# The first head pair's spectral weights in 4,096-byte rows of two modes, shared out over the slots anew, and the inverse transform's matrix made later

## The chip, the cores and the metric

The kernel runs on one core of a Trainium2 chip. The metric is the device time of one execution in microseconds. An execution that the hardware profiler took gives the profile; its span runs from the first to the last instruction of the program.

## The reference

Sliding-window attention with a linear bias per head feeds a spectral mixing layer:

```
scores = q @ k.T / 8 - slope[h] * |i - j|     kept where 0 <= i - j < 128
x = softmax(scores) @ v                       8 batches, 8 heads, 576 positions, 64 wide -> (8, 576, 512)
X = rfft(x, axis=1)[:, :64]                   64 modes
Y[b, m] = X[b, m] @ (w_r[m] + i w_i[m])       a 512 x 512 complex matrix for each mode
u = x + irfft(Y)
out = u + relu(u @ w_ch)
```

All inputs and the output are fp32. `w_r` and `w_i` have 64 x 512 x 512 elements each: 1 MiB for one mode of one of them, 134 MB in all, which is most of what the kernel reads.

## The kernel before, in words

Two heads are a pair: 128 of the 512 channels. A unit is one pair of one batch. `GROUPS` has two groups: pair 0 alone (8 units, one for each batch), then pairs 1, 2 and 3 together (24 units). Units are numbered 0 to 31 in this order. The program for each engine is in the order in which the code issues it; nothing is rescheduled.

The first stage is a run of slots, `_slot(g, n, w0, w1)`. In slot n PE does the scores of unit n (L407), the transposes of q and k of unit n + 1 (L381), a part of the modes' products (`w0`), the remaining scores, the spectrum of unit n - 2 (L502), then the attention-value product of unit n - 1 (L460), and last the other part of the modes (`w1`). ScalarE takes the exponentials (L419) and evicts the transposes (L389), VectorE multiplies by masks and normalizes, GpSimd casts q, k (L364) and v (L371) and issues the loads of v (L340). SyncE issues all other loads, in order: q and k of unit n + 8 in slot n (L329), and weights (L567).

The spectrum is a product with a matrix `F` of cosines and sines. Its result for a group goes to `X[j]`, with channels on partitions, in the three planes -imaginary, real, imaginary.

The products of pair 0 with its weights (`_modes`, L602 for `wr` and L606 for `wi`) run within the slots of the second group's attention and two slots (`TAIL`) behind them. A weight tile has three modes (22 tiles, the last with one): for a mode 128 rows of 512 fp32 elements, 2,048 contiguous bytes, one row to a partition. The tiles stand in a ring of three buffers for `wr` and three for `wi`. A tile is loaded when the tile three before it is used up; the load is issued in the same slot. The tiles are spread evenly from slot 10 on: one in each of slots 10 to 15, 17 to 21, 23 to 28 and 30 to 34. The result is added up in one PSUM tile for 8 modes, and ScalarE copies it to `ZTa` (L615).

`FT` is the matrix of the inverse transform, used only in the finish. `_ft(g, c)` makes a quarter of it: the first call transposes `F` (L308), scales it (L309), and each call makes a permutation `order` on GpSimd (L313), multiplies by it (L317) and evicts the result with ScalarE (L319). The calls stand behind slots 27 to 30.

Then comes the last stage: for each of 64 modes a tile with the rows of pairs 1, 2 and 3 (6,144 contiguous bytes to a partition, 768 KB for each of `wr` and `wi`), in the same ring; its products, and between them the transposes of x and x @ `w_ch` (`_xt` L628, `_xw` L637). The finish (`_finish`) applies `FT`, adds up and stores.

Of the kernel before, what the change touches and what calls it, by code (L numbers as in the profile page):

```python
# [9 lines left out]
FP32 = mybir.dt.float32  # L10
# [11 lines left out]
ROWS = 3  # L22
LV = 3
QK = 9
TAIL = 2


# [5 lines left out]
def kernel(  # L33
# [35 lines left out]


    g.FT = persist.tile([P, 4, S], BF16)
    g.ident_b = persist.tile([P, P], BF16)
    g.ident2 = persist.tile([P, 64], BF16)
    g.wch = persist.tile([P, 4, DM], BF16)
# [11 lines left out]
    with tc.manual_schedule(engines={ET.SP, ET.PE, ET.Activation, ET.DVE, ET.Pool}):  # L86
        with ExitStack() as wctx:
# [4 lines left out]
            with ExitStack() as actx:  # L92
                cp = actx.enter_context(tc.tile_pool(name="const", bufs=1))
                for j, grp in enumerate(GROUPS[:-1]):
                    g.X[j] = cp.tile([P, len(grp), 3, B, NM], BF16, name=f"X{j}")
                g.F = cp.tile([P, ST, P], BF16)
# [48 lines left out]

                line = [(j, *t) for j in range(len(GROUPS)) for t in tiles[j]]
                ahead = RING
                work = {n: [] for n in range(N + 2 + TAIL)}
                for j in range(len(GROUPS) - 1):
                    per = g.first[j + 2] - g.first[j + 1] + (TAIL if j + 2 == len(GROUPS) else 0)  # L150
                    for i, t in enumerate(tiles[j]):
                        work[g.first[j + 1] + 2 + i * per // len(tiles[j])].append((j, *t))
                for n in range(3, N + 2 + TAIL):
                    if g.first[1] <= n and loaded < N:
                        _load_unit(g, loaded)
                        loaded += 1
                    w = work[n]
                    for _ in w:
                        _load_w(g, *line[ahead])
                        ahead += 1  # L160
                    h = (len(w) + 1) // 2
                    _slot(g, n, w[:h], w[h:])
                    if N - 5 <= n < N - 1:
                        _ft(g, n - N + 5)
                    for i in range(2):
                        if n == g.first[1] + 4 + 4 * i:
                            _load_wch(g, i)
                        if n == g.first[1] + 6 + 4 * i:
                            _cast_wch(g, i)
# [8 lines left out]
            with ExitStack() as xctx:  # L178
# [30 lines left out]
def _consts(g, tp):  # L209
# [13 lines left out]
    for vb in g.vbs:  # L223
        nc.gpsimd.memset(vb[:, :, g.D : g.D + 1], 1.0)
    nc.gpsimd.memset(g.vbt[:, :, :, g.D : g.D + 1], 1.0)


    pcol = tp.tile([P, 1], FP32)
# [41 lines left out]
        nc.vector.tensor_tensor(out=r, in0=r, in1=o, op=ALU.max)  # L270
    nc.vector.tensor_scalar(off, rel, float(P), FAR, op0=ALU.is_ge, op1=ALU.mult)
    nc.vector.tensor_tensor(out=rel, in0=rel, in1=off, op=ALU.max)
    for s in range(g.NP):
        nc.vector.memset(slope[0:64, s : s + 1], -(2.0 ** (-8.0 * (2 * s + 1) / g.H)))
        nc.vector.memset(slope[64:128, s : s + 1], -(2.0 ** (-8.0 * (2 * s + 2) / g.H)))
# [15 lines left out]
    return 3 if k == c else c if k == 3 else k  # L291


def _ft(g, c):


    nc = g.nc
    S = g.S
    if c == 0:
        cvec = g.work.tile([P, 1], FP32, tag="cvec", name="cvec", bufs=1)  # L300
# [3 lines left out]
        g.FTn = g.work.tile([P, S], BF16, tag="FTn", name="FTn", bufs=1)  # L304
        for st in range(g.ST):
            n = min(P, S - st * P)
            tp = g.ps1.tile([P, P], BF16, tag="tqk", name="tft")
            nc.tensor.transpose(tp[:, 0:n], g.F[0:n, st], g.ident_b[0:n, 0:n])  # L308
            nc.vector.tensor_scalar_mul(g.FTn[:, st * P : st * P + n], tp[:, 0:n], cvec)  # L309
    order = g.work.tile([P, P], BF16, tag="order", name="order", bufs=1)  # L310
    src = g.ident_b.rearrange("p (r g m) -> p g r m", r=2, g=4)
    for k in range(4):
        nc.gpsimd.tensor_copy(  # L313
            order[:, 32 * k : 32 * k + 32].rearrange("p (r m) -> p r m", r=2), src[:, _block(c, k)])
    for a, z in ((0, 512), (512, S)):
        ps = g.ps1.tile([P, 512], FP32, tag="sc", name="ftp")
        nc.tensor.matmul(  # L317
            ps[:, 0 : z - a], lhsT=order, rhs=g.FTn[:, a:z], start=True, stop=True)
        nc.scalar.copy(g.FT[:, c, a:z], ps[:, 0 : z - a])  # L319
# [158 lines left out]
def _spectrum(g, n):  # L478
# [10 lines left out]
    po = 64 * (b % 2)  # L489
    ps = slice(po, po + 64)  # L490
    X = g.X[j]
    nb = 4 // A
    if b % nb == 0:
        g.xt = g.ps2.tile([P, nb, A, 2, g.NM], FP32, tag="xt", name="xt")
# [10 lines left out]
    if b % nb == nb - 1:  # L505
# [5 lines left out]
        for a in range(A):  # L511
            xi = xt[:, :, a].rearrange("p b i m -> p i b m")
            nc.vector.tensor_copy(X[:, a, 1:3, b0 : b0 + nb], xi)
            nc.vector.tensor_scalar_mul(X[:, a, 0, b0 : b0 + nb], xi[:, 1], -1.0)


def _slot(g, n, w0, w1):
# [32 lines left out]
        _spectrum(g, n - 2)  # L550
    if 0 <= n - 1 < N:
        _av(g, n - 1)
    if n < N:
        _mask3(g, n)
    for w in w1:
# [3 lines left out]
def _load_w(g, j, m0, mg):  # L559
# [3 lines left out]
    t = []  # L563
    for tag, src in (("wr", g.w_r), ("wi", g.w_i)):
        w = g.wpool.tile([P, ROWS, g.DM], FP32, tag=tag, name=f"{tag}{j}_{m0}")
        w = w[:, 0 : mg * A].rearrange("p (m a) e -> p m a e", a=A)
        nc.sync.dma_start(  # L567
            out=w.rearrange("p m a e -> p m (a e)"),
            in_=src[m0 : m0 + mg, rows].rearrange("m (p a) e -> p m (a e)", a=A))
        t.append(w)  # L570
    for i in range(mg):
        g.W[j, m0 + i] = (t[0][:, i], t[1][:, i])

# [12 lines left out]
def _modes(g, j, m0, n, last=False):  # L586
# [3 lines left out]
    X = g.X[j]  # L590
    A = len(GROUPS[j])
    ends = set(range(MB, g.NM + 1, MB)) | ({g.NM - 4, g.NM - 2} if last else set())
    for m in range(m0, m0 + n):
        if m == 0 or m in ends:
            g.acc[j] = (m, g.mpsum.tile([P, 4, 2, MB, 8], FP32, tag="acc", name="acc"))
# [20 lines left out]
        else:  # L616
            o = dst
            if last:
                o = g.ZT[:, :, c0 // 16, :, c0 % 16 : m % 16 + 1, :].rearrange(
                    "p e a m b -> p e a (m b)")  # L620
            nc.vector.tensor_tensor(out=o, in0=acc, in1=dst, op=ALU.add)


def _xt(g, n, pool, psum):
# [183 lines left out]
```

## Time and the profile before

| | |
|---|---|
| median of 3 runs | 493.46 us (493.18 to 494.25) |
| profiled execution | 492.82 us, span 491.1 us, mean granted clock of TensorE 0.782 |
| busy in the span | PE 372.5, VectorE 232.7, ScalarE 186.7, GpSimd 150.0 us |
| moved | 173.99 MB, 354 GB/s mean |
| weight transfers | 85 + 85 of 768 KB, 1 + 1 of 256 KB |

In the slices of the profile each digit is the busy share of an engine in tenths; PEclk is the clock that TensorE was granted, in tenths of full speed; DMA is the mean busy share of the core's 16 DMA engines. In the stretches the numbers behind an engine are busy microseconds and instructions, then come the granted clock, the DMA share (two queues that overlap can make it more than 1) and GB/s. In SyncE's waits the numbers are the microseconds in all, how often, and the longest.

### The profile page before, as it was taken

To read this page: it belongs to the slowest core of one execution; us is meant where nothing else is said; L and a number is where in the kernel's file an instruction comes from. 1 tells how busy PE (TensorE), PEld (TensorE's weight loads), DVE (VectorE), ACT (ScalarE), POOL (GpSimd) and SP (SyncE) were. 2 spreads that over 40 slices of the span, in tenths; PEclk is the share of its full clock that TensorE was granted. 3 is DMA by queue.
4 is the path that set the end of the run, shared out by engine and by line. 5 is a ranking of instruction groups with operands and counts; after the bars stand their busy time and mean duration, and the time that the engine had idled before them with its cause. 6 is when DMAs were issued, how large, how long until landed. Compare 5 with 4: busy or idle time off the path is not lost.

```text
span 491.1 us, 14883 instructions
## 1 busy us (share of the span) xinstructions
PE 372.5 (76%) x6415; PEld 252.9 (52%) x6415; DVE 232.7 (47%) x494; ACT 186.7 (38%) x343; POOL 150.0 (31%) x230
## 2 busy tenths in 40 slices
PE   2585787697677878777878798778868798845983
PEld 2464676576566756544544454444435455523542
DVE  8487663755745655532333334233332343202984
ACT  3694654655555547221111221222111132102772
POOL 8798673392935423000000000000000000000995
PEclk9988775967767569578787778888798788555999
DMA  8999999999999975799999999999999999992677
GB/s 251 299 295 283 328 291 350 355 363 343 362 377 311 361 294 178 247 410 424 423 423 423 424 423 423 423 424 418 420 415 424 423 424 421 424 423 104 223 288 258
DMA packets 54050, 173.99 MB, mean 354 GB/s; under 512 B 5600, under 2 KB 5600, under 8 KB 53984
## 3 DMA queue, kind: packets, MB, share of 16 engines
q1 hardware_dynamic: 50528, 163.60, 87.6%
q0 software_dynamic: 3456, 9.44, 7.4%
q8 instruction: 50, 0.82, 0.6%
q14 instruction: 16, 0.13, 0.1%
HBM read 163.58 MB, written 9.44 MB: 352 GB/s over the span
## 4 chain that ended last, share of the span: by engine, by line
DMA 60%; PE 25%; issue 6%; DVE 3%; ACT 3%; POOL 1%; SPq 1%; DVEq 0%; ACTq 0%; POOLq 0%
DMA wi<-in_moe_w_i_dram 53%; PE sc L407 5%; PE av L460 4%; DMA q<-in_q_dram 3%; PE acc L606 3%; PE xt L502 3%; DMA wchf<-in_moe_w_ch_dram 3%; PE acc L602 3%; PE tqk L381 3%; PE mm L637 2%; PE tp L628 1%; DVE r L766 1%; POOL o L774 1%; ACT att L419 1%; PE y L637 1%
## 5 line engine op out<-in xcount | busy, mean ns | idle before, releaser
L774 POOL TENSOR_TENSOR o<-r,ys 128x512 f32<-128x512 f32 x25 | 30.8, 1266 | 262.6 <-ACT ys L765 262.6
L655 ACT CAST hl<-xw 128x512 bf16<-128x512 f32 x72 | 42.1, 585 | 154.5 <-PE xw L637 150.2
L637 PE MATMUL xw<-wch,xT 128*64 128x512 bf16 x576 | 93.8, 465 | 0.0
L419 ACT ACTIVATE att<-sc 128x512 bf16<-128x512 f32 (+1 forms) x128 | 72.4, 592 | 53.8 <-PE sc L407 53.3
L606 PEld LDWEIGHTS <-wi 128*128 128x128 bf16 x1024 | 65.8, 103 | 52.1 <-DMA wi<-in_moe_w_i_dram 47.1
L602 PEld LDWEIGHTS <-wr 128*128 128x128 bf16 x1024 | 67.1, 103 | 40.4 <-issue 24.7
L656 DVE TENSOR_TENSOR hl<-xw,hl 64x512 bf16<-64x512 f32 x72 | 50.0, 695 | 79.3 <-ACT hl L655 79.3
L606 PE MATMUL acc<-Xlast,wi 128*128 128x16 bf16 x768 | 55.3, 193 | 37.1 <-DMA wi<-in_moe_w_i_dram 37.1
L422 DVE TENSOR_TENSOR att<-att,mask 128x512 bf16<-128x512 bf16 x96 | 46.9, 510 | 52.2 <-ACT att L419 51.6
L407 PE MATMUL sc<-qkT,qkT 64*64 64x256 bf16 (+1 forms) x512 | 56.9, 335 | 16.6 <-ACT att L419 5.9
L602 PE MATMUL acc<-Xlast,wr 128*128 128x16 bf16 x768 | 59.4, 193 | 12.7 <-DMA wr<-in_moe_w_r_dram 10.1
L637 PEld LDWEIGHTS <-xT 128*64 128x64 bf16 x576 | 37.9, 132 | 38.8 <-issue 22.0
L407 PEld LDWEIGHTS <-qkT 64*64 64x64 bf16 x512 | 33.8, 131 | 26.4 <-issue 18.4
L381 PE MATMUL tqk<-ident_b,qkb 64*64 64x64 bf16 x1152 | 34.0, 216 | 15.2 <-POOL qkb L364 8.0
L389 ACT COPY qkT<-tqk 128x576 bf16<-128x576 bf16 x64 | 41.1, 645 | 6.3 <-PE tqk L381 6.3
L381 PEld LDWEIGHTS <-qkb 64*64 64x64 bf16 x1152 | 34.1, 131 | 16.5 <-POOL qkb L364 8.6
L340 POOL DMA_DIRECT2D v<-in_v_dram x64 | 39.5, 622 | 0.8 <-POOL vb L371 0.8
L630 DVE COPY xT<-tp 128x512 bf16<-128x512 bf16 x36 | 15.3, 424 | 46.3 <-PE tp L628 45.9
L460 PE MATMUL av<-vb,att 64*128 64x65 bf16 (+1 forms) x1024 | 34.6, 221 | 3.3 <-issue 2.4
L460 PEld LDWEIGHTS <-att 64*128 64x128 bf16 (+1 forms) x1088 | 29.2, 116 | 8.3 <-issue 3.8
L371 POOL CAST vb<-v 128x512 bf16<-128x512 f32 x32 | 21.1, 658 | 39.3 <-PE av L460 37.9
L364 POOL CAST qkb<-q 128x576 bf16<-128x576 f32 x32 | 24.7, 771 | 6.4 <-PE tqk L381 4.9
(104 smaller groups left out, 486.4 us busy)
## 6 DMA issues: line engine op xcount, KB each, us to landing
wr<-in_moe_w_r_dram SPq DMA_DIRECT2D x85, 768.0 KB, 8.3
wi<-in_moe_w_i_dram SPq DMA_DIRECT2D x85, 768.0 KB, 9.7
q<-in_q_dram SPq DMA_DIRECT2D x32, 288.0 KB, 11.7
k<-in_k_dram SPq DMA_DIRECT2D x32, 288.0 KB, 11.4
v<-in_v_dram POOLq DMA_DIRECT2D x64, 128.0 KB, 7.3
out_dram<-o SPq DMA_DIRECT2D x32, 256.0 KB, 2.3
vt<-in_v_dram POOLq DMA_DIRECT2D x8, 128.0 KB, 8.2
wchf<-in_moe_w_ch_dram SPq DMA_DIRECT2D x2, 512.0 KB, 15.1
```

Source lines behind the costliest of these rows:

```text
L340: g.nc.gpsimd.dma_start(out=u.v[64 * hh : 64 * hh + 64].rearrange("p t r d -> p t (r d)"), in_=g.v[b, 2 * s + hh, 0:512, :].rearrange("(t ...
L381: g.nc.tensor.transpose(tp[hs, r, :], u.b[w][hs, r], g.ident_b[hs, hs], tile_position=(64 * hh, 64 * hh))
L389: g.nc.scalar.copy(dst.rearrange("c (p r) -> c p r", r=g.R), u.tp[w].rearrange("c r p -> c p r"))
L407: nc.tensor.matmul(sc[hs, r * nq : (r + 1) * nq], lhsT=kT[hs, kt * P + r : kt * P + P : 2], rhs=qT[hs, kt * P : kt * P + nq], start=True, ...
L419: nc.scalar.activation(a[:, :cols], sc[:, :cols], AF.Exp, scale=1.0 / math.sqrt(g.D))
L422: nc.vector.tensor_tensor(out=a, in0=a, in1=g.mask[:, s], op=ALU.mult)
L460: nc.tensor.matmul(av[o, hh, col(t)], lhsT=a[hs, c0 : c0 + m], rhs=vb[hs, 0 : D + 1], start=(j == 0), stop=(j == len(terms) - 1), tile_pos ...
L602: nc.tensor.matmul(o, lhsT=wr[:, a].bitcast(BF16)[:, 1::2][:, c], rhs=X[:, a, 1:3, :, m], start=(a == 0), stop=False)
L606: nc.tensor.matmul(o, lhsT=wi[:, a].bitcast(BF16)[:, 1::2][:, c], rhs=X[:, a, 0:2, :, m], start=False, stop=(a == A - 1))
L637: nc.tensor.matmul(out[64 * h : 64 * h + 64], lhsT=lhsT[h], rhs=rhs[h], tile_position=(0, 64 * h), **kw)
L655: nc.scalar.copy(hl, xw)
L656: nc.vector.tensor_tensor(out=hl[64:128], in0=xw[64:128], in1=hl[64:128], op=ALU.subtract)
```

## The change

Three things change. First, the weights of pair 0 come as 32 tiles instead of 22. A tile has modes m and m + 32, and one transfer of 512 KB for each of `wr` and `wi` brings both: the even partitions hold mode m, the odd ones mode m + 32, and each partition has two neighbouring channels' rows, 4,096 contiguous bytes. The product contracts over all 128 partitions at once, so `X[0]` gets a form with zeros: for each of the two modes, the partitions of the other one are zero, and the result has 32 columns (two modes, real and imaginary, 8 batches) instead of 16. A tile has 16 products for two modes, as before. Since a channel's spectrum now has to stand on an even and on an odd partition, a product with a permutation `swap` exchanges neighbouring partitions, and `_place` writes both versions, multiplied by 0 or 1 (`par`), on VectorE and ScalarE; this is done twice, in slots 5 and 9, for four batches each. `ZTa` is filled by two copies for each four tiles.

Second, the tiles are shared out otherwise: a weight of 4 for each slot up to 23 and of 7 from slot 24 on. One tile goes to each of slots 10 to 20, 22, 23, 25, 28, 30, 33 and 35, two to each of slots 24, 26, 27, 29, 31, 32 and 34.

Third, the four calls of `_ft` move from behind slots 27 to 30 to the last stage, behind its tiles 4 to 7; `F` is kept for that long, and the PSUM buffers are those of that stage.

```diff
+SHARE, SHARE_END = 4, 7
...
-        tiles.append([(m, min(mg, NM - m)) for m in range(0, NM, mg)])
+        tiles.append([(m, min(mg, NM - m)) for m in range(0, NM, mg)] if len(grp) > 1 else
+                     [(m, 2) for m in range(NM // 2)])
...
-                    per = g.first[j + 2] - g.first[j + 1] + (TAIL if j + 2 == len(GROUPS) else 0)
+                    steps = []
+                    for n in range(g.first[j + 1] + 2, g.first[j + 2] + 2):
+                        steps += [n] * (SHARE if n < N - LA else SHARE_END)
+                    if j + 2 == len(GROUPS):
+                        steps += [n for n in range(N + 2, N + 2 + TAIL)] * SHARE_END
+                    steps.sort()
                     for i, t in enumerate(tiles[j]):
-                        work[g.first[j + 1] + 2 + i * per // len(tiles[j])].append((j, *t))
+                        work[steps[i * len(steps) // len(tiles[j])]].append((j, *t))
...
-                    if N - 5 <= n < N - 1:
-                        _ft(g, n - N + 5)
...
+                    if 5 <= done < 9:
+                        _ft(g, done - 5, xt, xps)
...
+def _spectrum_swap(g, j, b):
+
+    sw = g.ps1.tile([P, 4, 2, g.NM], FP32, tag="sc", name="sw")
+    g.nc.tensor.matmul(
+        sw.rearrange("p b r m -> p (b r m)"), lhsT=g.swap,
+        rhs=g.xn.rearrange("p b r m -> p (b r m)"), start=True, stop=True)
+    _place(g, j, b - 3, sw, 1)
+
+
+def _place(g, j, b0, src, d):
+
+
+    nc = g.nc
+    n = g.NM // 2
+    for i in range(2):
+        o = g.X[j][:, i ^ d, i, :, :, b0 : b0 + 4]
+        x = src[:, :, :, n * i : n * i + n].rearrange("p b r m -> p r m b")
+        if i == 0:
+            nc.vector.tensor_scalar_mul(o[:, 1:3], x, g.par[:, 0:1])
+            nc.vector.tensor_scalar_mul(o[:, 0], x[:, 1], g.par[:, 2:3])
+        else:
+            nc.scalar.mul(o[:, 1:3], x, g.par[:, 1:2])
+            nc.scalar.mul(o[:, 0], x[:, 1], g.par[:, 3:4])
...
+        if A == 1:
+            w = w[:, 0:2]
+            nc.sync.dma_start(
+                out=w.rearrange("p a e -> p (a e)"),
+                in_=src[m0 : m0 + g.NM // 2 + 1 : g.NM // 2, rows].rearrange(
+                    "m (p a) e -> p m (a e)", a=2))
+            t.append(w)
+            continue
...
+def _modes_pair(g, j, m0):
...
+    if m0 % 4 == 0:
+        g.acc[j] = g.mpsum.tile([P, 4, 2, 2, 4, 8], FP32, tag="acc", name="acc")
...
+        for a in range(2):
+            for w, r in ((wr, 1), (wi, 0)):
+                nc.tensor.matmul(
+                    acc[:, et, :, :, m0 % 4], lhsT=w[:, a].bitcast(BF16)[:, 1::2][:, c],
+                    rhs=X[:, a, :, r : r + 2, m0],
+                    start=(a == 0 and r == 1), stop=(a == 1 and r == 0))
+    if m0 % 4 == 3:
+        for i in range(2):
+            m = i * g.NM // 2 + m0 - 3
+            dst = g.ZTa[:, :, :, m : m + 4].rearrange("p e r m b -> p e r (m b)")
+            src = acc[:, :, i].rearrange("p e r m b -> p e r (m b)")
+            if j == 0:
+                nc.scalar.copy(dst, src)
```

More of the change, by code (lines that the diff above doesn't have):

```diff
@@ L71 @@
     g.FT = persist.tile([P, 4, S], BF16)
+    g.F = persist.tile([P, ST, P], BF16)
     g.ident_b = persist.tile([P, P], BF16)
@@ L94 @@
                 for j, grp in enumerate(GROUPS[:-1]):
-                    g.X[j] = cp.tile([P, len(grp), 3, B, NM], BF16, name=f"X{j}")
-                g.F = cp.tile([P, ST, P], BF16)
+                    shape = [2, 2, 3, NM // 2, B] if len(grp) == 1 else [len(grp), 3, B, NM]
+                    g.X[j] = cp.tile([P, *shape], BF16, name=f"X{j}")
+                g.swap = cp.tile([P, P], BF16)
+                g.par = cp.tile([P, 4], FP32)
                 g.mask = cp.tile([P, NP, 512], BF16)
@@ L225, in _consts @@
     nc.gpsimd.memset(g.vbt[:, :, :, g.D : g.D + 1], 1.0)
+    nc.gpsimd.tensor_copy(
+        g.swap.rearrange("p (a i) -> p i a", i=2)[:, 0],
+        g.ident_b.rearrange("p (a i) -> p i a", i=2)[:, 1])
+    nc.gpsimd.tensor_copy(
+        g.swap.rearrange("p (a i) -> p i a", i=2)[:, 1],
+        g.ident_b.rearrange("p (a i) -> p i a", i=2)[:, 0])
     pcol = tp.tile([P, 1], FP32)
@@ L272, in _consts @@
     nc.vector.tensor_tensor(out=rel, in0=rel, in1=off, op=ALU.max)
+    odd = tp.tile([P, 1], I32)
+    nc.vector.tensor_single_scalar(odd, pi, 1, op=ALU.bitwise_and)
+    nc.vector.tensor_copy(g.par[:, 1:2], odd)
+    nc.vector.tensor_scalar(g.par[:, 0:1], g.par[:, 1:2], -1.0, 1.0, op0=ALU.mult, op1=ALU.add)
+    nc.vector.tensor_scalar_mul(g.par[:, 2:4], g.par[:, 0:2], -1.0)
     for s in range(g.NP):
@@ L291, in _block, with _ft @@
     return 3 if k == c else c if k == 3 else k
-def _ft(g, c):
+def _ft(g, c, pool, psum):
     nc = g.nc
@@ L299, in _ft @@
     if c == 0:
-        cvec = g.work.tile([P, 1], FP32, tag="cvec", name="cvec", bufs=1)
+        cvec = pool.tile([P, 1], FP32, tag="cvec", name="cvec", bufs=1)
         nc.vector.memset(cvec, 2.0 / S)
@@ L303, in _ft @@
         nc.vector.memset(cvec[64:65], 1.0 / S)
-        g.FTn = g.work.tile([P, S], BF16, tag="FTn", name="FTn", bufs=1)
+        g.FTn = pool.tile([P, S], BF16, tag="FTn", name="FTn", bufs=1)
         for st in range(g.ST):
             n = min(P, S - st * P)
-            tp = g.ps1.tile([P, P], BF16, tag="tqk", name="tft")
+            tp = psum.tile([P, 4, P], BF16, tag="tp", name="tft")[:, 0]
             nc.tensor.transpose(tp[:, 0:n], g.F[0:n, st], g.ident_b[0:n, 0:n])
             nc.vector.tensor_scalar_mul(g.FTn[:, st * P : st * P + n], tp[:, 0:n], cvec)
-    order = g.work.tile([P, P], BF16, tag="order", name="order", bufs=1)
+    order = pool.tile([P, P], BF16, tag="order", name="order", bufs=1)
     src = g.ident_b.rearrange("p (r g m) -> p g r m", r=2, g=4)
@@ L315, in _ft @@
     for a, z in ((0, 512), (512, S)):
-        ps = g.ps1.tile([P, 512], FP32, tag="sc", name="ftp")
+        ps = psum.tile([P, g.DM], FP32, tag="xw", name="ftp")
         nc.tensor.matmul(
@@ L491, in _spectrum @@
     X = g.X[j]
+    if A == 1:
+        _spectrum_pair(g, j, b)
+        return
     nb = 4 // A
@@ L514, in _spectrum, with _spectrum_pair @@
             nc.vector.tensor_scalar_mul(X[:, a, 0, b0 : b0 + nb], xi[:, 1], -1.0)
+def _spectrum_pair(g, j, b):
+    nc = g.nc
+    c0 = GROUPS[j][0] * P
+    po = 64 * (b % 2)
+    ps = slice(po, po + 64)
+    if b % 4 == 0:
+        g.xt = g.ps2.tile([P, 4, 2, g.NM], FP32, tag="xt", name="xt")
+    xt = g.xt
+    for st in range(g.ST):
+        l = g.x_sb[:, b, st, c0 : c0 + P] if st < 4 else g.x4[ps, b // 2, c0 : c0 + P]
+        f = g.F[:, st] if st < 4 else g.F[ps, st]
+        kw = {} if st < 4 else dict(tile_position=(po, 0))
+        nc.tensor.matmul(
+            xt[:, b % 4].rearrange("p r m -> p (r m)"), lhsT=l, rhs=f,
+            start=(st == 0), stop=(st == g.ST - 1), **kw)
+    if b % 4 == 3:
+        g.xn = g.work.tile([P, 4, 2, g.NM], BF16, tag="xn", name="xn", bufs=1)
+        nc.vector.tensor_copy(g.xn, xt)
+        _place(g, j, b - 3, xt, 0)
+def _spectrum_swap(g, j, b):
[5 more added lines that the diff above has]
+def _place(g, j, b0, src, d):
+    nc = g.nc
+    n = g.NM // 2
[8 more added lines that the diff above has]
+            nc.scalar.mul(o[:, 0], x[:, 1], g.par[:, 3:4])
 def _slot(g, n, w0, w1):
@@ L552, in _slot @@
         _av(g, n - 1)
+    if 0 <= n - 2 < N:
+        j, s, b = g.units[n - 2]
+        if len(GROUPS[j]) == 1 and b % 4 == 3:
+            _spectrum_swap(g, j, b)
     if n < N:
@@ L565, in _load_w @@
         w = g.wpool.tile([P, ROWS, g.DM], FP32, tag=tag, name=f"{tag}{j}_{m0}")
+        if A == 1:
+            w = w[:, 0:2]
[5 more added lines that the diff above has]
+            continue
         w = w[:, 0 : mg * A].rearrange("p (m a) e -> p m a e", a=A)
@@ L570, in _load_w @@
         t.append(w)
+    if A == 1:
+        g.W[j, m0] = t
+        return
     for i in range(mg):
@@ L592, in _modes @@
     ends = set(range(MB, g.NM + 1, MB)) | ({g.NM - 4, g.NM - 2} if last else set())
+    if A == 1:
+        _modes_pair(g, j, m0)
+        return
     for m in range(m0, m0 + n):
@@ L621, in _modes @@
             nc.vector.tensor_tensor(out=o, in0=acc, in1=dst, op=ALU.add)
+def _modes_pair(g, j, m0):
+    nc = g.nc
+    X = g.X[j]
+    if m0 % 4 == 0:
+        g.acc[j] = g.mpsum.tile([P, 4, 2, 2, 4, 8], FP32, tag="acc", name="acc")
+    acc = g.acc[j]
+    wr, wi = g.W.pop((j, m0))
+    for et in range(4):
+        c = slice(et * P, (et + 1) * P)
+        for a in range(2):
+            for w, r in ((wr, 1), (wi, 0)):
+                nc.tensor.matmul(
+                    acc[:, et, :, :, m0 % 4], lhsT=w[:, a].bitcast(BF16)[:, 1::2][:, c],
[8 more added lines that the diff above has]
+                nc.scalar.copy(dst, src)
+            else:
+                nc.vector.tensor_tensor(out=dst, in0=src, in1=dst, op=ALU.add)
 def _xt(g, n, pool, psum):
```

## The prediction, made before the changed kernel was run

> **What bounds the kernel now.** I read the page's slices first, then the stretches of the trace cut at the slots, then SyncE's waits, then the instructions of one slot. The slices show three stages:
>
> ```profile
> PE   2585787697677878777878798778868798845983
> ...
> PEclk9988775967767569578787778888798788555999
> DMA  8999999999999975799999999999999999992677
> GB/s 251 299 295 283 328 291 350 355 363 343 362 377 311 361 294 178 247 410 424 423 423 423 424 423 423 423 424 418 420 415 424 423 424 421 424 423 104 223 288 258
> ```
>
> One slice is 12.3 us. The DMA engines are full from the start to slice 13, fall to 7, 5 and 7 tenths in slices 14 to 16, are full at 423 GB/s to slice 35, and the last four slices are the finish. So transfers are the limit everywhere but in slices 14 to 16 and in the finish. An AV product, line L460, of unit n-1 closes slot n, so its end times cut the stretches: slots 10 to 23, 24 to 27, 28 to 31, the rest of the first pair, and the three other pairs:
>
> ```profile
> core 0: us, PE busy (x) PEld busy (x) DVE busy (x) ACT busy (x) POOL busy (x), PEclk, DMA share, GB/s
> 64.10:149.50 85.40, 66.34 (x1580) 55.77 (x1576) 46.80 (x123) 46.24 (x87) 47.78 (x73) 0.73 1.05 348
> 149.50:177.40 27.90, 22.89 (x481) 18.84 (x480) 16.30 (x37) 14.65 (x28) 12.06 (x23) 0.65 1.04 351
> 177.40:201.60 24.20, 18.52 (x421) 14.46 (x420) 13.38 (x42) 14.67 (x31) 6.05 (x17) 0.78 0.59 208
> 201.60:208.40 6.80, 5.55 (x105) 4.12 (x105) 3.50 (x10) 0.01 (x1) 0.00 (x0) 0.50 0.78 242
> 208.40:448.00 239.60, 189.16 (x2622) 110.79 (x2622) 76.48 (x127) 47.40 (x81) 0.00 (x0) 0.78 1.00 416
> ```
>
> Two queues overlap, so a full DMA reads 1.05 here. The third stretch loses 24.2 x (1.05 - 0.59) / 1.05 = 10.6 us of transfer time and the fourth 6.8 x (1.05 - 0.78) / 1.05 = 1.7 us: 12.3 us in which weights could have come. Why they did not is in SyncE's waits between 170 and 215 us:
>
> ```profile
> SPq L567 <- PE acc L606: 21.8, 6, 9.8
> SPq L567 <- PE sc L407: 12.3, 3, 7.8
> ```
>
> L567 is the load of a weight tile. It waits, up to 9.8 us at a time, for the mode products (L606) that free one of three ring buffers. Q and K loads ended with slot 23, so weights are all that is left to load, and PE is late with the tiles: slots 28 to 31 also hold the FT steps:
>
> ```profile
> 177.34 0.39 PE L308 MATMUL tft<-ident_b,F 128*128 128x128 bf16 x2
> ...
> 179.55 0.46 PE L308 MATMUL tft<-ident_b,F 128*128 128x128 bf16 x2 [1.82 <-DVE FTn L309]
> ...
> 181.65 0.64 PE L407 MATMUL sc<-qkT,qkT 64*64 64x256 bf16 x4 [0.62 <-ACT FT L319]
> ```
>
> From the end of the AV products at 177.4 to the next score at 181.65 the first FT step takes PE 4.2 us; the other three take 1.2, 1.4 and 1.1 (read in the same way). Together 7.9 us.
>
> **The change, part by part.** *Rows of 4,096 bytes.* The trace keeps each DMA packet with its size: the median is 84 ns for 2,048 bytes, 99 for 2,304 (q, k) and 234 for 6,144 (other pairs). The first pair's weights are 64 modes x 256 rows = 16,384 packets: x 84 ns / 16 engines = 86.0 us. Afterwards there are 8,192. No packet of 4,096 bytes of this queue is in the trace; halfway between 84 and 234 is 159 ns. The v queue has packets of that size: fastest 159, median 253.5, for those run beside q, k and weights. I take 159, since 84 and 234 are of the same queue: 8,192 x 159 / 16 = 81.4 us, **-4.6 us**. For the range: two short packets, 168 ns, give nothing; 253.5 gives +43.8; and as the mean of the short packet is 93.9, some may be saved beyond the median, up to another 5 us.
>
> Neighbouring rows now lie 32 MiB apart. The transfers of before take three modes, 1 MiB apart, in one transfer at 84 ns a row, 390 GB/s on 16 engines, and show no harm. The Trainium skill (DMA: Bandwidth & Descriptors, Latency and other measured facts) speaks against the change: row pitches of 4 and 8 MiB fell to 103 GB/s where a padded pitch reached 214. An estimate from that page takes 159 ns to 159 x 214 / 103, some 330: +88 us on the forecast, a time near 571. I follow the 84 ns.
>
> *Smaller tiles, shared out otherwise.* 22 tiles of three modes become 32 of two. Slots 10 to 23 had 36 modes and get 26; slots 24 to 35 had 28 and get 38. Transfers per stage, with 1.344 us a mode before (256 x 84 / 16), 1.272 after, q and k 256 x 99 / 16 = 1.58 us and v 64 packets x 245 (their mean) / 16 = 0.98 us a unit: slots 10 to 23 before, 36 x 1.344 + 14 x (1.58 + 0.98) = 84.2 us, against 85.4 measured, so the ledger holds. After: 26 x 1.272 + 35.8 = 68.9 us, 4.9 a slot. PE is busy 66.34 / 14 = 4.7 a slot there, and a slot whose waits are short takes 2.8 to 4.5 us from one AV end to the next, some 2.2 more with a spectrum (L502), every third time. So transfers stay the limit, barely; slot 24 begins some 15 us earlier.
>
> Slots 24 to 31 after: 13 tiles x 2.544 + 3 x 0.98 = 36 us of transfers. PE was busy 22.89 + 18.52 = 41.4 us in them, of which FT is about 3; six and a half tiles at 0.73 us (24 products at 30 ns pitch) become 13 at about 0.55 (16 products of 32 columns, pitch 30 to 37 ns): +2.4. So PE needs some 41 us, and transfers idle about 5 there. Slots 32 to 35 load 6 tiles, 15.3 us, over PE work of some 7: transfers lead. Adding 1 us for slots 3 to 23, where cover is thin, 6 us of idle transfers stay of the 12.3: **-6.3 us**. Bounds: none stays (-12.3), all stays (0).
>
> *FT late.* All that the four steps issue leaves slots 27 to 30: on PE five transposes and eight products, on ScalarE eight copies of 427 ns that stood before exponentials, on VectorE five scalings of 274 ns, on GpSimd 16 copies of some 209 to 260 ns, past casts of q, k, v; no DMA. Its gain is in the -6.3. They go behind tiles 4 to 7 of the last stage, where PE idles 239.6 - 189.2 = 50 us, so about 0.8 us per tile of 3.7. PE falls behind by 7.9 - 4 x 0.8 = 4.7 us at most, and two loads queued ahead cover 7.4. I take **+0.5 us**; without that cover 4.7.
>
> *The zeroed spectrum.* Twice (slots 5 and 9): on PE one 512-column product, about 0.4 us; on VectorE a cast of 692 ns and four multiplications for 692 + 415 before, about +1.0; on ScalarE four of 128 or 256 columns, some 0.3 each by the 586 ns of 512, +1.2. A score waits for the `sc` buffer that the swap borrows. Next are the exponentials of the next slot; the DMA, at 1.05, hides it. At the start two GpSimd copies of about 0.25 us (`order`'s take 209) stand before the first v load and the cast at 4.25 us, and four small VectorE operations of 0.15. The modes' copies to `ZTa` (ScalarE, 586 ns x 8) become 16 of half the width, about 0.35: +0.9 spread out. Taken: **+0.3**; uncovered about 5.
>
> *The number of transfers* rises from 44 to 64 and their size falls from 768 to 512 KB, so the ring holds 3 MB, not 4.5. In the last stage 768 KB transfers follow each other at a share of 1.00, so nothing fixed is paid per transfer there.
>
> Sum on the profiled execution (span 491.1, itself 492.8): 492.8 - 4.6 - 6.3 + 0.5 + 0.3 = 482.7. The median of the runs, 493.46, is 0.64 above it: **483.3 us**. The last 239.6 us of weights and the finish keep their length; they begin earlier.
>
> **Rivals.** *A, PE keeps the idle:* modes are moved into slots where PE is late already, and a lower clock (0.65 in slots 24 to 27, 0.50 behind) eats what FT gives back. All 12.3 us stay: 492.8 - 4.6 + 0.8 + 0.6 = 489.6. For: PE is busy 41.4 of 52.1 us there. Against: 7.9 us of FT go.
>
> *B, transfers full to the end of the pair:* idle nought, rows as reckoned: 483.3 - 6.0 = 477.3; with shorter packets in the busy stage as low as 472. For: the third stretch has PE busy only 77% of its time. Against: the tile pace of 1.6 a slot needs slots of 4.5 us.
>
> *C, slower, by the packet:* rows 32 MiB apart collide and a 4,096-byte packet costs as much as v's 253.5 ns. 43.8 us in place of the -4.6 gives 532. It decides from where the other terms, -5.5, are eaten: 168 + 5.5 x 16 / 8.192 = 179 ns. For: no row of that pitch in the trace. Against: the three modes 1 MiB apart.
>
> *D, no change:* A with packets of two times 84 ns: 494.2.
>
> **How the numbers follow.** The forecast 0.54 (its own range 479 to 487), A 0.16, B 0.15, C 0.10, D 0.05. A difference under about 0.2%, 1 us, can't be told from none. Faster: 0.54 + 0.16 + 0.15 = 0.85, of which I move 0.01 to slower for PE falling further behind in the last stage; same 0.03 and slower 0.02 from D, so slower 0.13. The range 474 to 491 leaves out C, most of D and the lowest end of B, some 0.17.
>
> **What would show it.** Right: 4,096-byte packets near 159 ns; a share of 1.05 to about slot 24, a dip shallower than 0.59 behind it; the last stage begins near 198 us and runs 239 to 241 us at 1.00; L567's waits for mode products there under half. Wrong: packets over 179 ns, a last stage over 243 us with shares under 1.00 at its tiles 4 to 8, or a dip as deep as now.

## The result, and the profile after

The changed kernel takes 497.03 us (median of 20 runs) against 493.40 for the kernel before (20 runs): a ratio of 1.0072, interval 1.005 to 1.0094. It is slower by 3.6 us, where 10 us less were forecast. The profiled execution took 497.2 us, its span is 495.4.

Two measures are used below beside the views. The *idle* of the transfers is read from the trace's packet records: the time in which fewer than 16 packets were under way, in units of all 16 engines, from 5 us to the last stage. It gives some 12 us before (12.2 below, good to about 0.4), as the stretches did (12.3). The *begin* of the last stage is reckoned back from its first 600 packets of 6,144 bytes at 234 ns; its *end* is when the last one has landed.

The slices of the page after (PE, its clock, DMA, GB/s):

```profile
PE   3484867788774867477978788888888799855984
PEclk9998769775797897568797877778887879655998
DMA  8999979999999897999999999999999999994677
GB/s 253 296 272 262 308 210 267 344 338 343 347 308 321 317 350 280 410 425 422 362 379 412 420 425 418 418 424 418 418 423 424 417 415 415 424 421 178 216 288 263
```

The dip of slices 14 to 16 is shallower, as meant (9, 7 and 9 tenths in place of 7, 5 and 7). A new one stands at slice 5 (210 GB/s), and slices 19 and 20, early in the last stage, fall to 362 and 379 GB/s. Cut at the AV products, as before (slots 10 to 23, 24 to 27, 28 to 31, the rest of the pair, the last stage):

```profile
core 0: us, PE busy (x) PEld busy (x) DVE busy (x) ACT busy (x) POOL busy (x), PEclk, DMA share, GB/s
67.40:146.00 78.60, 61.35 (x1507) 50.68 (x1507) 51.35 (x124) 47.98 (x94) 47.33 (x72) 0.75 0.98 310
146.00:172.60 26.60, 18.56 (x483) 15.54 (x478) 16.53 (x36) 13.33 (x26) 11.95 (x18) 0.81 0.96 314
172.60:193.50 20.90, 16.57 (x429) 13.47 (x430) 11.93 (x35) 12.81 (x26) 3.41 (x5) 0.84 0.88 316
193.50:207.40 13.90, 6.66 (x147) 4.96 (x145) 4.17 (x12) 0.71 (x3) 0.00 (x0) 0.69 1.00 374
207.40:452.40 245.00, 191.99 (x2633) 111.71 (x2629) 77.38 (x133) 50.36 (x90) 2.64 (x16) 0.77 1.00 413
```

Slot 24 begins at 146.0 us, 3.5 us earlier than before, not 15. Unit 30's AV product ends 8.1 us earlier, at 193.5, but the weights are behind by then: the pair's last ones keep the DMA full for another 13.9 us. The last stage begins at 207.4 (before 205.6) and lasts 245.0 us (before 241.3): +1.8 and +3.7 us. Of the 9.3 us of idle 4.4 lie around slot 10 (60 to 80 us) and 4.5 in slots 24 to 31, close to the 5 that the prediction left there.

Where slice 5 comes from, by PE and ScalarE around slot 10:

```profile
67.34 0.61 PE L569 MATMUL sw<-xn,swap 128*128 128x512 bf16 x1
67.88 0.64 PE L430 MATMUL sc<-qkT,qkT 64*64 64x256 bf16 x4
70.41 0.63 PE L430 MATMUL sc<-qkT,qkT 64*64 64x256 bf16 x4 [1.89 <-ACT X L588]
70.79 1.21 PE L404 MATMUL tqk<-ident_b,qkb 64*64 64x64 bf16 x36
71.94 0.21 PE L729 MATMUL acc<-X,wr 128*128 128x32 bf16 x1
```

```profile
67.94 0.47 ACT L587 ACTIVATE X<-xt,par 128x256 bf16<-128x256 f32 x1 [0.95 <-DVE X L585]
68.31 0.36 ACT L588 ACTIVATE X<-xt,par 128x128 bf16<-128x128 f32 x1
69.62 0.47 ACT L587 ACTIVATE X<-sw,par 128x256 bf16<-128x256 f32 x1 [0.95 <-DVE X L585]
70.00 0.36 ACT L588 ACTIVATE X<-sw,par 128x128 bf16<-128x128 f32 x1
70.25 0.60 ACT L442 ACTIVATE att<-sc 128x512 bf16<-128x512 f32 x1
```

VectorE, around the same time (lines between these are left out), and the two loads of SyncE between which it issues nothing:

```profile
67.51 0.34 DVE L585 TENSOR_SCALAR X<-xt,par 128x128 bf16<-128x128 f32 x1
68.00 0.69 DVE L492 TENSOR_TENSOR x_sb<-av,rec 128x512 bf16<-128x512 f32 x1
68.81 0.47 DVE L584 TENSOR_SCALAR X<-sw,par 128x256 bf16<-128x256 f32 x1
69.20 0.33 DVE L585 TENSOR_SCALAR X<-sw,par 128x128 bf16<-128x128 f32 x1
```

```profile
62.59 1.09 SPq L352 DMA_DIRECT2D k<-in_k_dram  x1
72.55 0.55 SPq L646 DMA_DIRECT2D wr<-in_moe_w_r_dram  x1
```

The placing takes 3.3 us (67.1 to 70.4) because its parts stand in a row. VectorE has the normalization of unit 8 (L492 and three shorter ones) between its two turns and does not wait here. ScalarE waits for VectorE in each turn, 0.95 us twice, though it writes other modes of `X`. Both read the same PSUM tile and write the same tile `X`; which of the two makes ScalarE wait is not shown. The second score waits for the buffer that the swap borrowed, and the first product of the modes starts at 71.9, 4.5 us behind the AV product of unit 8. In the kernel before it starts 1.6 us behind (AV's end at 64.1):

```profile
65.75 0.19 PE L602 MATMUL acc<-X,wr 128*128 128x16 bf16 x1
```

Until then no weight tile can be loaded, all q and k of the window are on their way, and three tiles hold only 3 MB: the DMA runs dry, 3.9 us of idle between 70 and 80 us.

Slices 19 and 20 are the FT steps:

```profile
226.00:232.00 6.00, 6.00 (x62) 2.96 (x58) 1.99 (x4) 1.76 (x3) 0.00 (x0) 0.72 1.02 426
232.00:237.00 5.00, 2.72 (x37) 1.49 (x34) 2.59 (x10) 1.28 (x3) 0.66 (x4) 0.92 1.01 416
237.00:241.00 4.00, 4.00 (x44) 2.32 (x44) 0.42 (x1) 1.01 (x3) 0.66 (x4) 0.50 0.87 324
241.00:247.00 6.00, 5.29 (x58) 2.57 (x56) 2.44 (x5) 2.15 (x5) 0.66 (x4) 0.83 0.95 367
247.00:252.00 5.00, 4.00 (x72) 2.70 (x70) 1.79 (x3) 1.69 (x4) 0.00 (x0) 1.00 0.85 324
```

PE is busy without a gap before the first step (226 to 232), so it is behind already when FT arrives; the transposes then wait 1.9 us for VectorE, the granted clock is 0.50 for 4 us, and the DMA share falls to 0.87 and 0.85: L653's loads wait for buffers that PE frees. The kernel before has such a stretch at about the same distance from the begin of its last stage (the third line here):

```profile
217.00:221.00 4.00, 2.03 (x33) 1.19 (x29) 1.39 (x2) 1.17 (x2) 0.00 (x0) 1.00 1.02 427
221.00:225.00 4.00, 2.56 (x35) 1.62 (x37) 0.42 (x1) 0.00 (x0) 0.00 (x0) 0.70 1.01 424
225.00:229.00 4.00, 4.00 (x52) 2.31 (x50) 1.81 (x3) 1.17 (x2) 0.00 (x0) 0.87 1.02 427
```

### The profile page after: what moved, and what is told of

It reads as the page before. It is cut to its first block, busy times and chain, and to the rows that moved or that the text cites. A ratio compares the mean times of both kernels' runs of the same rounds, so it can differ in the third digit from the quotient of the medians.

```text
span 495.4 us, 14951 instructions
## 1 busy us (share of the span) xinstructions
PE 366.2 (74%) x6417; PEld 245.7 (50%) x6417; DVE 240.9 (49%) x504; ACT 190.7 (38%) x359; POOL 150.8 (30%) x232
## 4 chain that ended last, share of the span: by engine, by line
DMA 45%; PE 32%; issue 8%; DVE 6%; POOL 3%; ACT 3%; SPq 0%; POOLq 0%; ACTq 0%; DVEq 0%
DMA wi<-in_moe_w_i_dram 44%; PE sc L430 7%; PE av L483 4%; PE tqk L404 4%; PE xt L528 3%; PE acc L729 3%; PE acc L698 3%; PE xw L757 2%; PE acc L694 2%; DMA vt<-in_v_dram 2%; PE mm L757 1%; PE tp L748 1%; DVE r L886 1%; ACT att L442 1%; POOL v L363 1%
## 5 line engine op out<-in xcount | busy, mean ns | idle before, releaser
L757 PE MATMUL xw<-wch,xT 128*64 128x512 bf16 x576 | 95.6, 472 | 0.0
L445 DVE TENSOR_TENSOR att<-att,mask 128x512 bf16<-128x512 bf16 x96 | 53.7, 589 | 37.2 <-ACT att L442 36.7
L698 PEld LDWEIGHTS <-wi 128*128 128x128 bf16 x768 | 49.0, 103 | 38.7 <-DMA wi<-in_moe_w_i_dram 38.7
L694 PEld LDWEIGHTS <-wr 128*128 128x128 bf16 x768 | 50.1, 103 | 36.1 <-issue 22.2
L430 PE MATMUL sc<-qkT,qkT 64*64 64x256 bf16 (+1 forms) x512 | 54.9, 328 | 13.3 <-ACT att L442 5.0
L404 PEld LDWEIGHTS <-qkb 64*64 64x64 bf16 x1152 | 32.3, 128 | 24.2 <-POOL qkb L387 12.1
L483 PE MATMUL av<-vb,att 64*128 64x65 bf16 (+1 forms) x1024 | 32.9, 212 | 12.4 <-issue 10.1
L430 PEld LDWEIGHTS <-qkT 64*64 64x64 bf16 x512 | 31.2, 127 | 21.1 <-issue 14.7
L483 PEld LDWEIGHTS <-att 64*128 64x128 bf16 (+1 forms) x1088 | 27.3, 109 | 19.9 <-issue 14.1
L729 PE MATMUL acc<-X,wi 128*128 128x32 bf16 x256 | 17.7, 181 | 11.3 <-DMA wi<-in_moe_w_i_dram 10.6
```

What stands on the lines that cost most here:

```text
L404: g.nc.tensor.transpose(tp[hs, r, :], u.b[w][hs, r], g.ident_b[hs, hs], tile_position=(64 * hh, 64 * hh))
L430: nc.tensor.matmul(sc[hs, r * nq : (r + 1) * nq], lhsT=kT[hs, kt * P + r : kt * P + P : 2], rhs=qT[hs, kt * P : kt * P + nq], start=True, ...
L445: nc.vector.tensor_tensor(out=a, in0=a, in1=g.mask[:, s], op=ALU.mult)
L483: nc.tensor.matmul(av[o, hh, col(t)], lhsT=a[hs, c0 : c0 + m], rhs=vb[hs, 0 : D + 1], start=(j == 0), stop=(j == len(terms) - 1), tile_pos ...
L694: nc.tensor.matmul(o, lhsT=wr[:, a].bitcast(BF16)[:, 1::2][:, c], rhs=X[:, a, 1:3, :, m], start=(a == 0), stop=False)
L698: nc.tensor.matmul(o, lhsT=wi[:, a].bitcast(BF16)[:, 1::2][:, c], rhs=X[:, a, 0:2, :, m], start=False, stop=(a == A - 1))
```

## The experiments

**Transfers alone.** A kernel that only loads: the first pair's weights in four forms of rows, then the same beside a stream of v.

> Transfers alone, no computation: the output is zeros. SyncE loads the first pair's weights as 2,048-byte rows (three modes a transfer), as 4,096-byte rows of modes m and m + 32, as 4,096-byte rows of modes 2i and 2i + 1, then the other pairs' 6,144-byte rows, some 17 MB each; then the same four again while GpSimd loads v in 256 KB steps. Theory P (proportional: a second queue slows a packet by its bytes): alone 84, 159, 159 and 234 ns a packet, 390 to 423 GB/s; beside v the two- and four-kilobyte stretches move within 3% of the same GB/s, the long packet near 205 ns, the short one near 105. Rival H (32 MiB between neighbouring rows is slow): the stretch of m and m + 32 is over 5% slower than that of neighbouring modes, alone or beside v. Rival L (the long rows themselves suffer from v): both stretches of 4,096 bytes are over 5% slower than that of 2,048 beside v.

Stretches within each form, in the order of the expectation; the last four are beside v. The two busy times in each line are those of VectorE and GpSimd:

```profile
10.00:47.70 37.70, 0.00 (x0) 0.00 (x0) 1.00 1.05 388
48.90:88.60 39.70, 0.00 (x0) 0.00 (x0) 1.00 1.03 410
89.90:129.80 39.90, 0.00 (x0) 0.00 (x0) 1.00 1.03 410
130.00:171.00 41.00, 0.00 (x0) 0.00 (x0) 1.00 1.02 417
182.00:238.00 56.00, 0.00 (x0) 17.17 (x28) 1.00 1.05 324
239.60:300.40 60.80, 0.00 (x0) 18.46 (x32) 1.00 1.03 331
302.80:365.30 62.50, 0.00 (x0) 18.36 (x30) 1.00 1.03 326
366.00:410.00 44.00, 0.00 (x0) 12.27 (x20) 1.00 1.02 327
```

Alone, rows of 4,096 bytes bring 410 GB/s against 388: the 6% of the forecast. Beside v all forms move 324 to 331 GB/s, v included, and the packets' means are 100.4 and 192.5 ns: theory P, by the total. But v does not get the same share in each: 70 GB/s beside the short rows, 64 and 63 beside the long ones. The weights by themselves get 254, 268 and 263, so long rows still bring them 4 to 6% more, partly at v's expense. Rows 32 MiB or 1 MiB apart differ by nothing alone and 2% the wrong way beside v: rival H is out, and so is rival L.

**Rows alone, neighbours, and FT.** Three kernels.

`short_rows`: tiles of two modes in rows of 2,048 bytes, with the sharing out and the late FT.

```diff
 # the kernel before, with SHARE, SHARE_END = 4, 7 and the late _ft of the changed kernel, and
-        mg = ROWS // len(grp)
+        mg = 2 if len(grp) == 1 else ROWS // len(grp)
```

> The changed kernel's tile size (two modes, 512 KB), sharing out 4 to 7 and late FT, but the kernel before's rows of 2,048 bytes of modes 2i and 2i + 1, without swap, zeros and placing. Theory P: long rows save nothing where v and q, k run beside them, so the time is that of the changed kernel within 0.6%, 494 to 500. The forecast's own step (159 against 168 ns for the same bytes): 4.6 us slower than the changed kernel, 501 to 502. Rival H (pitch) or S (the spectrum's swap delays slots 5 and 9): 3 us or more faster, under 494.

It took 492.28 us (ratio to the kernel before 0.9968, 0.9943 to 0.9993), 4.7 us *faster* than with long rows. By the expectation this is the case of S or H: something that the long rows bring with them costs time, not their packets alone. The next runs part the two. In `short_rows` the first product of the modes comes 1.5 us behind unit 8's AV, and the transfers idle 1.4 us between 60 and 80 us, against 4.4.

`neighbours`:

```diff
-                in_=src[m0 : m0 + g.NM // 2 + 1 : g.NM // 2, rows].rearrange(
+                in_=src[2 * m0 : 2 * m0 + 2, rows].rearrange(
 # and the spectrum's and ZTa's columns to match
```

> The changed kernel with modes 2i and 2i + 1 in a tile in place of m and m + 32: the neighbouring rows are 1 MiB apart instead of 32 MiB. ZTa is filled by four copies for each four tiles, not two. Theory P: 4,096-byte packets stay at a mean of 183 to 195 ns, the time within 0.5% of the changed kernel, 495 to 500. Rival H: the mean falls to 170 or less and the time by 5 us or more, to 492 or less.

495.46 us, packets at 186 to 195 ns in slots 10 to 27. No fall to 492: H is out in the kernel too.

`ft_early`:

```diff
+                    if N - 5 <= n < N - 1:
+                        _ft(g, n - N + 5)
 ...
-                    if 5 <= done < 9:
-                        _ft(g, done - 5, xt, xps)
```

> The changed kernel with the four FT steps back behind slots 27 to 30 (FTn stands in the buffer of w_ch's loads, for want of space). Theory P with F (FT late costs what the last stage grew by): the last stage shrinks from 246.6 to 242 to 243 us; slots 28 to 31 get 5 to 8 us longer, of which the transfers lose 2 to 6, as the ring covers 7.6 us; together 493 to 499. Rival T (FT late is the whole loss against the forecast): 484 to 490.

495.82 us. The last stage is back to its old length:

```profile
209.30:450.70 241.40, 188.83 (x2615) 110.89 (x2615) 75.99 (x125) 47.47 (x82) 0.00 (x0) 0.78 1.01 419
```

245.0 to 241.4 us: FT behind tiles 4 to 7 costs 3.6 us there. Slots 28 to 31 lengthen by 3.3 us to 24.2, less than the 5 to 8 expected; the begin of the last stage moves from 207.4 to 209.3. FT alone is not the loss (rival T is out).

**The swap, and FT apart.**

`no_swap`:

```diff
-            _spectrum_swap(g, j, b)
 ...
+                    nc.gpsimd.memset(g.X[0], 0.0)
```

> The changed kernel without the swap product and the four multiplications that place its result (zeros stand in their place, set by GpSimd at about 12 us while it waits for v): half of the first pair's spectrum is left out. Theory S (the swap and the placing, one after the other, hold the scores of slots 6 and 10 by about 2 us each, and as the ring has only 3 MB the transfers run dry at slot 10): the first modes' product starts 2 to 4 us earlier behind the AV product of unit 8, the idle of the transfers between 60 and 80 us falls from 4.4 us to 1 to 2, and the time falls by 2 to 4 us, to 493 to 495. Rival R (long rows themselves are the loss against short_rows, by their packets): within 1 us of the changed kernel, 496 to 498.

492.81 us, 4.2 us off the changed kernel. The stretch that was dry, in the changed kernel and then without the swap:

```profile
70.00:76.00 6.00, 5.59 (x142) 5.10 (x142) 3.01 (x8) 4.45 (x10) 2.78 (x5) 0.52 0.46 133
```

```profile
70.00:76.00 6.00, 4.68 (x128) 4.10 (x128) 3.02 (x10) 3.45 (x8) 3.26 (x5) 0.72 1.03 339
```

A share of 0.46 becomes 1.03, the idle between 60 and 80 us falls from 4.4 to 1.2 us, and the first product starts 1.6 us behind the AV product of unit 8 in place of 4.5. Theory S holds, and without the swap long rows and short ones (492.28) can't be told apart.

`short_ft_spread` (in the kernels named `..._ft_spread` the edit is the same):

```diff
-                    if 5 <= done < 9:
-                        _ft(g, done - 5, xt, xps)
+                    if done in (12, 20, 28, 36):
+                        _ft(g, (done - 12) // 8, xt, xps)
```

> short_rows with the four FT steps behind tiles 12, 20, 28 and 36 of the last stage in place of 4 to 7. Theory F (four steps in a row make PE later than two loads cover; one step every eight tiles does not): the last stage falls from 245.6 us to 241.5 to 242.5, the time from 492.3 to 488 to 490, ahead of both kernels. Rival (the last stage is longer because more of the throttled clock falls in it, wherever FT stands): no gain, 491 to 493.

488.07 us, 4.2 less than `short_rows`; the last stage 241.6 us at a share of 1.01. So where the steps stand was the fault, not the stage. The edit moves them apart and later at once; which of the two helps was not tried.

`share_ft_late` and `ft_late_only` put the sharing out and the late FT, and the late FT alone, on the kernel before.

> The kernel before with the sharing out 4 to 7 and the late FT alone: tiles of three modes, rows of 2,048 bytes, ring of 4.5 MB. If the smaller ring (3 MB) costs something: 1 to 3 us faster than short_rows' 492.3, with the transfers never idle between 60 and 80 us. If it does not: 491.5 to 493.

> The kernel before with the late FT alone. By the forecast's step for FT (7.9 us of PE leave slots 27 to 30, where transfers idle): the idle before the last stage falls from 12.2 us to 5 to 8; the last stage grows from 241.4 to 245 as in the changed kernel; together 489 to 493. Rival (PE's lateness there is not FT's): idle stays at 10 to 12, time 495 to 498.

`ft_late_only`: 488.95 us. Idle 4.7 us, the last stage begins at 197.5 (8.1 us earlier) and takes 245.7 (4.4 more). The forecast's 7.9 us for what FT takes off slots 27 to 30 holds. `share_ft_late`: 490.37, with idle of only 2.1 us and no dry stretch at slot 10; the sharing out on top of the late FT gains nothing. It lies 1.9 us below `short_rows`, as expected if the smaller ring costs something, but the intervals of the two ratios overlap (0.9903 to 0.9964 and 0.9943 to 0.9993).

**The ladder.** The last two sets take the change apart one step at a time.

`ring4` put the ring of each weight into one buffer of nine rows, four tiles deep for the pair.

> The changed kernel with four tiles of the first pair in the ring's memory instead of three (4 MB in flight; the buffers of 6 KB had 2 KB spare each). Theory B (bytes in flight: the smaller tiles let the transfers run dry at slot 10 and single DMA engines run dry between): the idle between 60 and 80 us falls from 4.4 us to 1 or less, the mean of the 4,096-byte packets from 189 ns to 180 to 186, the time by 2 to 4 us, to 493 to 495. Rival: the swap's hold of slot 10 counts whatever the ring holds, since the tile loads wait for slot 10's products: idle stays at 3 to 4, time 496 to 498.

It took 645.91 us and tells nothing on the depth: its last weights land at 438 us and the products that use them end near 602. Why was not followed up.

> The changed kernel with the FT steps behind tiles 12, 20, 28 and 36 of the last stage in place of 4 to 7. Theory F, as in short_ft_spread: the last stage falls from 245 us to 241 to 242, the time from 497 to 492.5 to 493.5. Rival (the gain there was the earlier start of slot 10, not FT): 495 to 498.

`after_ft_spread`: 492.70 us, 4.3 less; the dry stretch of 70 to 76 us is still there (share 0.26), the last stage is 242.7 us. Over all profiles but `ring4`'s the last stage takes 241.3 to 241.7 us with FT in the slots (three kernels), 245.0 to 247.4 with FT behind tiles 4 to 7 (six), and 241.5 to 243.5 with FT spread (five), but 244.9 in a sixth, `no_swap_ft_spread`; why there is not known.

> The kernel before with FT alone moved, behind tiles 12, 20, 28 and 36 of the last stage. If ft_late_only's gain (8 us of earlier start, 4.3 us given back in the last stage) and the spread's add: last stage 241 to 242 us, time 484.5 to 486, the fastest of all. If the smaller tiles and the sharing out are needed for it: 488 to 490.

`before_ft_spread`: 484.05 us, the fastest of all; 8.3 us ahead of the kernel before by the ratio (0.9832, 0.9796 to 0.9868), 9.4 by the medians of the table below:

```profile
64.40:149.00 84.60, 67.81 (x1580) 57.11 (x1576) 48.16 (x122) 46.37 (x87) 47.60 (x73) 0.68 1.05 354
149.00:177.70 28.70, 23.50 (x484) 19.28 (x484) 16.20 (x37) 14.64 (x28) 11.89 (x19) 0.64 1.03 341
177.70:193.70 16.00, 14.35 (x404) 12.02 (x401) 10.91 (x34) 11.90 (x23) 3.72 (x5) 0.91 0.77 273
193.70:196.50 2.80, 1.91 (x62) 1.70 (x58) 1.96 (x6) 0.17 (x1) 0.00 (x0) 0.62 0.80 252
196.50:438.30 241.80, 189.70 (x2665) 112.88 (x2663) 79.57 (x139) 50.35 (x89) 2.63 (x16) 0.80 1.01 417
```

Slots 28 to 31 take 16.0 us in place of 24.2, and the rest of the pair up to the begin of the last stage 2.8 in place of 4.0 (201.6 to 205.6); the other stretches stay within 0.8 us.

> The kernel before with the sharing out 4 to 7 alone: three modes a tile, FT behind slots 27 to 30. By the forecast's step the later slots load more and idle less: idle 12.2 to 7 to 10 us, time 489 to 492. Rival (PE is late there because of FT, and takes tiles no faster for having more of them): the time within 1 us of the kernel before, 493 to 495.

`share_only`: 492.70 us (0.9981, 0.9951 to 1.0012). Idle falls to 9.5 us (in a profile 3.4 us under the median); the gain can't be told from none.

> before_ft_spread with the sharing out 4 to 7, in tiles of three modes. If more tiles in the late slots fill the idle that is left there (5.3 us): 481 to 483. If PE takes them no faster, as share_ft_late against ft_late_only showed (490.4 against 488.95): 484 to 486.

`share_ft_spread`: 486.97 us, above both ranges. Idle falls from 5.3 to 2.8 us and the time does not.

> The changed kernel without the swap and with FT behind tiles 12, 20, 28 and 36: half of the first pair's spectrum is left out. If the two losses found so far add (4.2 us and 4.3 us off 497): 488 to 489.5, the same as short_ft_spread (488.07) with rows of 2,048 bytes, and still 3 to 5 us behind before_ft_spread. If long rows gain once nothing else is in the way: 484 or less.

`no_swap_ft_spread`: 489.20 us. The two losses add as expected, and no gain from the long rows is seen.

```diff
 # two_ahead: before_ft_spread, and
-                ahead = RING
+                ahead = AHEAD        # 2; likewise for the tiles loaded ahead of the slots
```

> before_ft_spread (484.05 us) with the first pair's tiles loaded two ahead instead of three, so some 3 MB of weights in flight instead of 4.5; rows, tiles and the last stage's ring as there. Theory B (fewer bytes in flight let single DMA engines run dry, and the next packet takes longer): the 2,048-byte packets before the last stage rise from a mean of 93 to 95 to 97 ns, the idle from 5.3 us by 2 or more, the time to 486.5 to 490. Rival (the tile size or the shorter transfers do it, not the bytes in flight): within 1.5 us of before_ft_spread, 483 to 485.5.

`two_ahead`: 486.35 us, 2.3 more, just short of what theory B asked; the packets' mean is unchanged at 95.0 ns, the idle 6.1 us. Against the kernel before the two ratios are nearly the same (0.9843, 0.9815 to 0.9871, and 0.9832), so a cost of fewer bytes in flight is not shown; slower packets are not its way.

In steps from the fastest kernel to the changed one ("work" is the begin less the idle; begin and idle are from single profiles, whose own time lies up to 2.9 us from the median here):

| kernel | median us | step | begin | idle | work |
|---|---|---|---|---|---|
| before (12 to 29 runs a set) | 493.4 to 494.3 | | 205.6 | 12.2 | 193.4 |
| `before_ft_spread` | 484.05 | FT out of the slots: -9.4 from 493.40 | 196.5 | 5.3 | 191.2 |
| `share_ft_spread` | 486.97 | sharing out: +2.9 | 197.9 | 2.8 | 195.1 |
| `short_ft_spread` | 488.07 | two modes a tile: +1.1 | 201.9 | 4.7 | 197.2 |
| `no_swap_ft_spread` | 489.20 | long rows, placing: +1.1 | 200.7 | 6.2 | 194.5 |
| `after_ft_spread` | 492.70 | swap: +3.5 | 207.5 | 10.3 | 197.2 |
| changed kernel | 497.03 | FT behind tiles 4 to 7: +4.3 | 207.4 | 9.3 | 198.1 |

The intervals of neighbouring rows overlap in the three middle steps, so none of these is shown by itself; their sum, 5.1 us from 484.05 (ratio 0.9796 to 0.9868) to 489.20 (0.9876 to 0.9939), is, though by the ratios it is 3.7 us. FT out of the slots and the swap are shown by two experiments each, the place of FT in the last stage by three (`short_rows`, `ft_late_only` and the changed kernel, each against its kernel with FT spread: 4.2, 4.9 and 4.3 us).

## Why the prediction was wrong

*What bounds the kernel*, and FT as the cause of the idle in slots 28 to 31, were right: the late FT alone begins the last stage 8.1 us earlier (7.9 read off PE), and FT alone, out of the slots and spread, gives -8.3 to -9.4 us, more than the -6.3 forecast for FT and the sharing out together.

*FT late*, +0.5 us: the step that failed is the cover, "PE idles 239.6 - 189.2 = 50 us, so about 0.8 us per tile", an average over a stage of 64 tiles. Just before the first step PE was busy without a gap for 6 us, so there was no idle to take; the kernel before showed the same at 225 to 229 us. In the steps PE waited 1.9 us for VectorE and had 4 us at a clock of 0.50, and the two loads queued ahead, reckoned as 7.4 us of cover, did not cover it. It cost 3.6 us of the last stage and 4.3 us of time, near the price that the text named without cover (4.7). Spread over later tiles most or all of it is covered. The text's own sign of being wrong, a last stage over 243 us with shares under 1.00 there, came.

*The zeroed spectrum*, +0.3 us: "the DMA, at 1.05, hides it" failed. Its operations were costed one by one, about 3 us; that ScalarE's part waits for VectorE's, and VectorE's second turn stands behind a normalization, was not seen, nor that the swap is the last thing ahead of slot 10's products, which free the ring. The smaller ring was told in the text and given no price; together they ran the DMA dry for 3.9 us. A ring of 3 MB alone does not: between 60 and 80 us `two_ahead`, with 3 MB in flight, has no idle, and `no_swap` 1.2 us. Measured: 4.2 us (`no_swap`), 3.5 with FT out of the way; the "uncovered about 5" was near.

*Rows*, -4.6 us: the packet of 4,096 bytes has a median of 159 ns, to the nanosecond. Its mean is 189.2, and twice the mean of the short rows before the last stage, 94.8, is 189.6. So by means the transfers take 96.9 us in place of 97.1: the term is -0.2, not -4.6. It compared medians, in a stage where q, k and v run beside the weights. The text had the short packet's mean, 93.9, in sight and put it on the side of a further gain. Its sign of 179 ns was reckoned from medians (168 ns for two short packets); by means they took 189.6 already.

*Sharing out and smaller tiles*, part of the -6.3 us: the idle of slots 24 to 31 came out as forecast (4.5 us, 5 forecast), but the ledger's 68.9 us for slots 10 to 23 became 78.6, and slot 24 began 3.5 us earlier, not 15. Slot 10 itself began 3.3 us later, which the ledger did not look at: at 66.1 to 68.6 us in all kernels with long rows, with the swap or without, and at 62.6 to 65.4 in those with three modes a tile (63.4 and 66.5 with short rows and two modes); why is not shown. Of the 9.7 us that the stretch is longer, 3.9 are the dry stretch. The rest is longer packets, not only of weights. The packets of slots 10 to 23, priced as in the ledger, took 9% more than that before and 16% more in the changed kernel, so that the ledger came out right before was in part luck (84.2 against 85.4 us, with packets that overlap). With rows of 2,048 bytes and three modes a tile, v's mean there is 224 to 236 ns in four kernels with the old sharing out and 233 to 239 in three with the new; the weights' mean is 92.5 to 93.4 and 93.9 to 95.2. The same v, q and k run in fewer microseconds beside the weights; that this is the cause is argued, not shown. In sum the sharing out, the smaller tiles and the long rows cost 5.1 us by the medians where the rows were to give 4.6. With FT out of the slots (-9.4), the swap (+3.5) and FT's place in the last stage (+4.3) that makes the measured +3.6 us, where the terms -4.6, -6.3, +0.5 and +0.3 were forecast.

By rivals: A, idle that stays, was near for the changed kernel (9.3 of 12 us), but half of it lies at slot 10, which A did not name. C's direction came true, its mechanism did not: the packet takes 163 ns alone (the mean in `packets`), and rows 32 MiB apart do no harm. The rule of the Trainium skill on row pitches (DMA: Bandwidth & Descriptors, Latency and other measured facts) describes another pattern, one large pitch from each partition to the next; this one, two streams 32 MiB apart, ran at 410 GB/s, the same as 1 MiB apart.

## What to carry to other kernels

Cover has to be read in the stretch where the moved work lands, and at the engine that would give it: a stage's average idle (50 us here) says nothing of its first tiles, and four steps in a row at its start cost 4.3 us that the same steps, later and spread out, did not. A "full" DMA hides a delay only while transfers are queued, so a change that makes the ring smaller and delays what frees the ring must be costed as one. When three edits come together, run each alone: FT out of the slots, and spread, is worth 8 to 9 us by itself, and the rest of the change gives 12 to 13 back. And a sum over packets goes by their mean.

## What the runs showed of the hardware that was not expected

Rows of 2,048, 4,096 and 6,144 bytes move 388, 410 and 417 GB/s alone but 324, 326 to 331 and 327 GB/s in all beside a v stream in 512-byte pieces: by the total the advantage of 4,096 bytes falls from 6% to 1 to 2%. The rows also change what v gets, 70 GB/s beside the short ones and 60 to 64 beside the longer, so the weights alone still gain 4 to 6%. And a packet's mean in the kernel lies 13% above its median for short rows (94.8 and 84 ns) and 19% for long ones (189.2 and 159), so medians flatter the longer row.
